# Polysketch attention into an ELU layer: the first keys in two loads of whole rows, the head in another order, sums read between the two ELU halves

## Chip, cores, metric

One core of one Trainium2 chip. The time is device microseconds for one execution of the whole program; the kernel before takes 302.09 us (median of 9 runs, 301.78 to 302.22).

## What is computed

```python
def phi(x):                                   # S1, S2: (8, 32)
    a = np.einsum('rd,bhsd->bhsr', S1, x)
    b = np.einsum('rd,bhsd->bhsr', S2, x)
    return np.einsum('bhsi,bhsj->bhsij', a, b).reshape(*x.shape[:-1], 64)
q_p, k_p = phi(q), phi(k)                     # q, k, v: (4, 4, 1088, 32)
kv  = np.einsum('bhsf,bhsd->bhfd', k_p, v)
z   = np.sum(k_p, axis=2)
x   = einsum('bhsf,bhfd->bhsd', q_p, kv) / (einsum('bhsf,bhf->bhs', q_p, z) + 1e-6)
x   = x.transpose(0, 2, 1, 3).reshape(4352, 128)
h   = x @ w_in                                # (128, 2048)
g   = where(h > 0, h, exp(min(h, 0)) - 1)
out = g @ w_out                               # (2048, 128)
```

Keys are summed over the whole sequence of a batch, so no query of a batch can be finished before all its keys are. S1, S2 and the two weight matrices arrive as 64-bit numbers and are turned into 32-bit ones on the chip.

## The kernel before

The 4352 tokens are 68 half tiles of 64. A *group* g holds eight of them (512 tokens; group 8 has half as many). The 2048 hidden columns are eight *pairs* cp of two 128-column blocks c. A *step* is one (group, pair).

**The loop.** In step n TensorE makes the hidden columns, `mm1(g, cp)` (L496, tile `h`, four buffers, two per step). ScalarE and VectorE make the ELU of each block: `elu_a` (two activations, L504 and L505, into `e`) and `elu_d` (L511, into `gg`). Two steps later `mm2` (L525) adds the pair's product into `o`, a tile with one buffer. After the last pair of a segment `fin1` reads `o` so that the next segment may write it: a ScalarE copy to `oT` (L538), a VectorE addition to `oT` (L534), or a VectorE transpose to `ob` (L545), followed by the stores. The groups 0 and 1 go in segments of pairs 0-1, 2-3 and 4-7, in turns, because their weights are still being prepared; each later group is one segment. The program is scheduled by hand: each engine executes its instructions in the order in which the code emits them. Attention work of the later batches and the preparation of later weights are put into given steps (`at` before the step's elu, `late` after it).

**Preparing weights.** A pair's 64-bit words are loaded to `raw` and turned into `W`, by `RA` (L101, VectorE), `RB` (L106, ScalarE) and `RC`, which is four VectorE passes: `round_c` (L114, L115), `round_d` (L119), `round_e` (L127; for later pairs two POOL passes, L124 and L125). Entry i of `order` says what is prepared: 0 is the w_in half of pair 0, 1 is all of pair 1, 2 is the w_out half of pair 0, 3 is pair 2, and so on.

**The head.** Before the loop, batch 0's keys are loaded (`hd_k`, L140-141), transposed in 32x32 blocks (`transp`, L247, to `kT`), and sent through: `KF` (feature matmuls L269, copy to `ab` L273), `KO` (outer product to `kp`, L253), `KA` (sums over the keys into `kv`, L296), `KC` (`kvz`, L307), `KZ1` (`zm`, L316) and `KZ2` (L323, L324: the sums of keys as query weights `SW`), `KS` (POOL copies to `kvS`, L331). `make_SX` (L242-243) makes a helper for `KZ2`. Each has three parts (key tiles 0-3, 4-7, 8) where a second index is given.

Group 0 of the queries has a path of its own, so as not to wait for `SW`: `q1_first` (L394), `q2_first`, `q4_first` (L411-412), `q5_first` (x0ps L427, then the division dn, xn L438-440, the transposes x0tp L445 and copies to `xg`, L447-448). Group 1 goes by the general path: `q1` (L363, copy to `abw` L368), `q2` (L375-384, ending with the outer product `qp`), `q4` (transposes L460, copies to `qpT` L461), `q5` (L475) and `q5_out` (copies to `xg`, L486 on ScalarE and L487 on VectorE). `keep_warm` (L216) is a matmul into a tile that nobody reads.

**Loads.** Nearly all are issued by SP in program order: the S matrices, k's first part, q's first half tiles, the w_in half of pair 0, v of batch 0 (two loads of 64 partitions), the rest of pairs 1 and 0, q's second part, then the further pairs and batches. ScalarE's queue takes S2 and k's second part.

The order of the head that the change rewrites is L566-611, and the loop's body L655-673.

Of the kernel before, what the change touches and what calls it, by code (L numbers as in the profile page):

```python
# [22 lines left out]
def _ap(ap: bass.AP, free):  # L23
    return dataclasses.replace(ap, ap=[list(ap.ap[0])] + [list(x) for x in free])
# [3 lines left out]
def kernel(  # L28
# [44 lines left out]
    def load_hd(eng, x, src, b, t0, t1):  # L73
        if (x, b) not in hd:
            hd[x, b] = work.tile([P, 2, NT, D], F32, name="hd_" + x, tag="hd_" + x)
        eng.dma_start(hd[x, b][:, :, t0:t1, :],
                      src[b].rearrange("h (a c t) d -> (h a) c t d", a=32, c=2)[:, :, t0:t1, :])

    def load_v(eng, b):
        for u in range(2):  # L80
            t0, t1 = u * KT, min(NT, u * KT + KT)
            r = slice(64 * u, 64 * u + 64)
            src = v[b].rearrange("h (y t) d -> y h t d", t=NT)[:, :, t0:t1, :]
            if b == 0:
                eng.dma_start(vt[b][r, :VN].rearrange("p (h t d) -> p h t d", h=H, t=KT)[:, :, :t1 - t0, :], src)
            else:
                for h in range(H):
                    eng.dma_start(vt[b][r, h * KT:h * KT + t1 - t0, :D], src[:, h])
# [45 lines left out]
    for x, (eng, src) in enumerate(((nc.sync, S1), (nc.scalar, S2))):  # L134
# [2 lines left out]
            eng.dma_start(raw_s[rs].rearrange("p c w -> p (c w)"), src.bitcast(U32))  # L137
        else:
            eng.dma_start(S16[rs, :], src)
    load_hd(nc.sync, "k", k, 0, 0, KT)  # L140
    load_hd(nc.scalar, "k", k, 0, KT, NT)
    warm = const.tile([R, 1], F32, name="warm")
    nc.vector.memset(warm[:], 0.0)
    nc.scalar.activation(warm[:], warm[:], EXP)
# [5 lines left out]
    def load_w(cp, i):  # L150

        f = slice(2 * cp * P, (2 * cp + 2) * P)
        src = moe_w_out[f, :].rearrange("(c p) d -> p c d", p=P) if i else moe_w_in[:, f]
        if wide:
            if cp not in raw_w:
                raw_w[cp] = work.tile([P, 4 * P, 2], U32, name="raw", tag="raw", bufs=6)
            src = src.bitcast(U32)
            to = raw_w[cp][:, 2 * P * i:2 * P * i + 2 * P, :].rearrange("p c w -> p (c w)")
        else:
            to = W[:, cp, 2 * P * i:2 * P * i + 2 * P]  # L160
        nc.sync.dma_start(to.rearrange("p (c f) -> p c f", f=src.shape[-1]) if i else to, src)
# [16 lines left out]
    def RC(i, pool=False):  # L178
        round_w(round_c, i)
        round_w(round_d, i)  # L180
        round_w(round_e, i, pool)

    load_w(0, 0)
    load_v(nc.sync, 0)
    load_w(1, 0)
    load_w(1, 1)
    load_w(0, 1)
    load_hd(nc.sync, "q", q, 0, 8, NT)
    for cp in range(2, NP):
        load_w(cp, 0)  # L190
        load_w(cp, 1)
# [34 lines left out]
    Sx = const.tile([2 * R, H, D], F32, name="Sx")  # L226
    nc.vector.tensor_copy(Sx[:], _ap(S16[:], [[0, H], [1, D]]))

    Sab = const.tile([FD, H, 2 * R], F32, name="Sab")
    SW = const.tile([FD, B, H, 3, R], F32, name="SW")  # L230
    keep_warm(3)
# [8 lines left out]
    def make_SX():  # L240
        xps = psum.tile([P, 512], F32, name="SXps", tag="aux")
        nc.tensor.matmul(xps[:, :FD], idr[:].rearrange("p x j -> p (x j)"), Sx[:R].rearrange("p h d -> p (h d)"))  # L242
        nc.scalar.copy(SX[:], xps[:, :FD])


    def transp(dst, x, b, t0, t1):
        nc.vector.transpose(dst[b][:, t0:t1, :].rearrange("p t (a c) -> p c t a", c=2), hd[x, b][:, :, t0:t1, :])  # L247


    def outer(dst, ab):  # L250
# [61 lines left out]
    def KZ1(b):  # L312

        zms[b] = work.tile([P, 2, 2, R], F32, name="zm", tag="zm")
        z_ = kvz[b][:, :, :, D] if b == 0 else kvz[b][:, :, 0, D:]
        (nc.vector if b == 0 else nc.gpsimd).tensor_mul(  # L316
            zms[b][:], _ap(z_, [z_.ap[1], z_.ap[2] if b == 0 else [0, 2], [0, R]]),
            _ap(zmask[:], [[0, 2], [R, 2], [1, R]]))

# [48 lines left out]
        nc.scalar.copy(abw[g][:, :H * n, :].rearrange("p (h t) y -> p h t y", h=H),  # L368
                       p[:, :n * 96].rearrange("p (t h y) -> p h t y", t=n, h=H))

    def q2(g):
        m = H * qn[g]
        x = abw[g][:, :m, :]
        pw = pws[g % 2]
        nc.vector.tensor_mul(pw[:, :m, :R], x[:, :, R:2 * R], x[:, :, 2 * R:])  # L375
        den = work.tile([P, 4 * H], F32, name="den", tag="den")
        nc.vector.tensor_reduce(den[:, :m], pw[:, :m], axis=AX, op=ADD)
        nc.vector.reciprocal(den[:, :m], den[:, :m])
        an = work.tile([P, 4 * H, R], F32, name="an", tag="an")
        nc.vector.tensor_mul(an[:, :m], x[:, :, R:2 * R], _ap(den[:, :m], [[1, m], [0, R]]))  # L380
        qp[g] = work.tile([P, 4 * H, R, R], F32, name="qp", tag="qp", bufs=2)
        a_ = an[:, :m]
        b_ = x[:, :, :R]
        nc.vector.tensor_mul(qp[g][:, :m], _ap(a_, list(a_.ap[1:]) + [[0, R]]),  # L384
                             _ap(b_, [b_.ap[1], [0, R], b_.ap[2]]))

# [25 lines left out]
    def q5_first():  # L414
        KC(0)
        KZ1(0)
        KS(0)
        round_w(round_c, 0)
        round_w(round_d, 0)
        keep_warm(2)  # L420
        xps = []
        for tt in range(2):
            p = psum.tile([P, 512], F32, name="x0ps", tag="h", bufs=4)
            xps.append(p[:, :8 * (D + 1)].rearrange("p (m d) -> p m d", d=D + 1))
            for m in range(4):
                t, g2 = 2 * tt + m // 2, m % 2
                nc.tensor.matmul(p[:, 2 * m * (D + 1):2 * (m + 1) * (D + 1)], qpT[0][:, t, g2, :],  # L427
                                 kvz[0][:, g2].rearrange("p w d -> p (w d)"), skip_group_check=True)
            if tt == 0:
                KZ2(0)  # L430
        round_w(round_e, 0)
        q1(1)
        keep_warm(1, P)
        dn = work.tile([P, 2, 8], F32, name="dn", tag="dn", bufs=1)
        xn = work.tile([P, 2, 8, D], F32, name="xn", tag="xn", bufs=1)
        xg[0] = work.tile([P, 512], F32, name="xg", tag="xg", bufs=2)
        for tt in range(2):
            nc.vector.tensor_scalar(dn[:, tt], xps[tt][:, :, D], 1e-6, None, op0=ADD)  # L438
            nc.vector.reciprocal(dn[:, tt], dn[:, tt])
            nc.vector.tensor_mul(xn[:, tt], xps[tt][:, :, :D], _ap(dn[:, tt], [[1, 8], [0, D]]))  # L440
        xt = []
        for tt in range(2):
            q = psum.tile([P, 512], F32, name="x0tp", tag="aux")
            for t in range(2):
                nc.tensor.transpose(q[:, t * P:t * P + P], xn[:, tt, 4 * t:4 * t + 4].rearrange("p m d -> p (m d)"), ident[:])  # L445
            xt.append(q)
        nc.scalar.copy(xg[0][:, :256], xt[0][:, :256])  # L447
        nc.vector.tensor_copy(xg[0][:, 256:], xt[1][:, :256])  # L448

    def q4(g):  # L450

# [37 lines left out]

    hs, es, gs, ops = {}, {}, {}, {}  # L490

    def mm1(g, cp):
        n = qn[g] * P
        hs[g, cp] = [psum.tile([P, 512], F32, name="h", tag="h", bufs=4) for c in range(2)]
        for c in range(2):
            nc.tensor.matmul(hs[g, cp][c][:, :n], W[:, cp, c * P:c * P + P], xg[g][:, :n])  # L496

    def elu_a(g, cp, c):

        n = qn[g] * P  # L500
        if c == 0:
            es[g, cp] = work.tile([P, 2, 512], F32, name="e", tag="e", bufs=2)
        e = es[g, cp][:, c, :n]
        nc.scalar.activation(e, hs[g, cp][c][:, :n], RELU, scale=-1.0)  # L504
        nc.scalar.activation(e, e, EXP, scale=-1.0)  # L505

    def elu_d(g, cp, c):
        n = qn[g] * P
# [2 lines left out]
        nc.vector.scalar_tensor_tensor(gs[g, cp][:, c, :n], es[g, cp][:, c, :n], -1.0, hs[g, cp][c][:, :n],  # L511
                                       op0=ADD, op1=MAX)

    def elu(g, cp):
        for c in range(2):
            elu_a(g, cp, c)
            elu_d(g, cp, c)

    def mm2(g, cp, first, last):
        n = qn[g] * P  # L520
# [43 lines left out]


    keep_warm(2)  # L566
    transp(kT, "k", 0, 0, KT)
    transp(kT, "k", 0, KT, NT)
    KF(0, 0)
    transp(qT, "q", 0, 0, 8)  # L570
    q1_first()
    KO(0, 0)
    KF(0, 1)
    KF(0, 2)
    q2_first()
    RA(0)
    RB(0)
    KO(0, 1)
    KO(0, 2)
    RA(1)  # L580
    RA(2)
    KA(0, 0)
    q4_first()
    make_SX()
    KA(0, 1)
    RB(1)
    RB(2)
    KA(0, 2)
    transp(qT, "q", 0, 8, NT)
    q5_first()  # L590
    mm1(0, 0)
    round_w(round_c, 1)
    round_w(round_d, 1)
    round_w(round_e, 1)
    for c in range(2):
        elu_a(0, 0, c)
    q2(1)
    mm1(0, 1)
    elu_a(0, 1, 0)
    for c in range(2):  # L600
        elu_d(0, 0, c)
    q4(1)
    round_w(round_c, 2)
    q5_out(1, q5(1, True))
    elu_a(0, 1, 1)
    round_w(round_d, 2)
    round_w(round_e, 2)
    for c in range(2):
        elu_d(0, 1, c)
    RA(3)  # L610
    RB(3)


# [41 lines left out]
    for n in range(N + 4):  # L655
        if 2 <= n < N:
            g, cp, first, last = steps[n]
            mm1(g, cp)
        for f, *a in extra.get(n, ()):
            f(*a)  # L660
        if 2 <= n < N:
            elu(g, cp)
        for f, *a in extra.get((n, 1), ()):
            f(*a)
        if 2 <= n < N + 2:
            g, cp, first, last = steps[n - 2]
            mm2(g, cp, first, last)
            if last:
                fin1(g, cp == NP - 1)
                if cp == NP - 1 and g == NQ - 1:  # L670
                    done[n + 2] = g
        if n in done:
            fin2(done[n])

# [28 lines left out]
```

## Time and profile before

| | us |
|---|---|
| median of 9 runs | 302.09 |
| the profiled execution | 301.81 |
| its span, first to last instruction | 299.5 |
| first key-feature matmul (L269) | 6.69 |
| last key-sum matmul, start of `kvz` (L307) | 14.29, 14.34 |
| first mm1 (group 0, pair 0) | 19.75 |
| first mm1 of the loop (group 1, pair 0) | 28.03 |
| last mm2 | 292.06 to 294.67 |

"Before" is one profiled execution; times are microseconds from the start of the span. A row of the chain of waits gives start, duration, engine, output tile, line and, behind an x, how many records were merged. A 32-bit matmul instruction leaves two records. `PEld` is TensorE's loading of weights, `SPq` the issuing of a DMA. In the slices of the page a digit is the busy share in tenths of 7.5 us. In a table by stretch the columns are busy time (and records) of PE, PEld, DVE, ACT and POOL, then the granted clock, the DMA share and GB/s. In the rows of one tile, three durations in ns are the least, the median and the greatest.

### The profile page before, as it was taken

Reading aid. Unit: us, or ns where it says so; the run is one execution under the profiler, and the core shown is the slowest. Engines: PE = TensorE matmul, PEld = TensorE weight load, DVE = VectorE, ACT = ScalarE, POOL = GpSimd, SP = SyncE. Lnnn points to the kernel's source line nnn. Section 1 sums busy time; section 2 is a strip of 40 time slices with the busy share of each in tenths; the row PEclk is TensorE's granted clock in tenths of the full one; section 3 lists DMA queues with packets and bytes.
Section 4 is the critical chain, followed back from the end, with each engine's and each line's share of the span. In section 5 each row is a group of like instructions: output and inputs, shape, how many; then the busy total and the mean of one; then the engine's idle time right before and its main releaser. Section 6 shows DMA issues by size and latency. Waiting matters only on the chain.

```text
span 299.5 us, 4046 instructions
## 1 busy us (share of the span) xinstructions
PE 287.8 (96%) x1454; PEld 147.5 (49%) x1454; DVE 168.7 (56%) x297; ACT 188.2 (63%) x354; POOL 18.5 (6%) x45
## 2 busy tenths in 40 slices
PE   8887999999998999999998999999999999999994
PEld 5763344544454653444544654445444544444682
DVE  5778899963765384436456175435433644354441
ACT  1536888566666268746657368656774687568581
POOL 2010034530000010000000010000000000000000
PEclk9999999999999999999999999999999999999999
DMA  6932999220010100001000200001001000110020
GB/s 191 335 120 77 205 215 215 30 74 0 9 29 0 28 10 0 2 10 26 2 1 6 31 0 0 0 14 23 0 0 24 14 0 1 15 23 0 4 32 18
DMA packets 38291, 13.37 MB, mean 45 GB/s; under 512 B 32768, under 2 KB 36480, under 8 KB 38272
## 3 DMA queue, kind: packets, MB, share of 16 engines
q1 hardware_dynamic: 37984, 12.86, 19.2%
q8 instruction: 11, 0.18, 0.3%
q10 hardware_dynamic: 288, 0.26, 0.3%
q14 instruction: 8, 0.07, 0.1%
HBM read 10.88 MB, written 2.23 MB: 44 GB/s over the span
## 4 chain that ended last, share of the span: by engine, by line
PE 92%; ACT 3%; DVE 3%; issue 1%; DVEq 0%
PE o L525 39%; PE h L496 37%; PE kv L296 3%; PE xps L475 2%; PE idle L216 2%; PE qtp L460 2%; PE abp L269 2%; PE abwp L363 2%; ACT e L505 1%; ACT e L504 1%; ACT ab L273 1%; PE x0ps L427 1%; DVE qp L384 0%; PE abqp L394 0%; DVE gg L511 0%
## 5 line engine op out<-in xcount | busy, mean ns | idle before, releaser
L511 DVE SCALAR_TENSOR_TENSOR gg<-e,h 128x512 f32<-128x512 f32 (+1 forms) x144 | 93.0, 655 | 105.8 <-ACT e L505 105.6
L525 PE MATMUL o<-gg,W 128*128 128x512 f32 (+1 forms) x288 | 130.7, 577 | 1.3 <-ACT oT L538 0.7
L496 PE MATMUL h<-xg,W 128*128 128x512 f32 (+1 forms) x288 | 128.8, 569 | 1.7 <-DVE xg L448 0.6
L504 ACT ACTIVATE e<-h 128x512 f32<-128x512 f32 (+1 forms) x144 | 81.5, 566 | 25.4 <-PE h L496 24.9
L505 ACT ACTIVATE e<-e 128x512 f32<-128x512 f32 (+1 forms) x144 | 87.3, 606 | 4.6
L496 PEld LDWEIGHTS h<-xg,W 128*128 128x128 f32 x288 | 54.5, 190 | 65.1 <-issue 55.9
L525 PEld LDWEIGHTS o<-gg,W 128*128 128x128 f32 x288 | 52.2, 190 | 54.8 <-issue 46.4
L368 ACT COPY abw<-abwp 128x384 f32<-128x384 f32 (+1 forms) x8 | 3.7, 459 | 28.4 <-PE abwp L363 28.4
L461 ACT COPY qpT<-qtp 128x512 f32<-128x512 f32 (+1 forms) x16 | 8.2, 562 | 17.1 <-PE qtp L460 17.1
L253 DVE TENSOR_TENSOR kp<-ab 128x1024 f32<-128x1024 f32 (+1 forms) x12 | 11.0, 943 | 5.8 <-ACT ab L273 5.8
L273 ACT COPY ab<-abp 128x256 f32<-128x256 f32 (+1 forms) x12 | 3.8, 317 | 12.9 <-PE abp L269 12.6
L296 PEld LDWEIGHTS kv<-v,kp 128*64 128x64 f32 (+1 forms) x288 | 9.1, 137 | 2.6 <-issue 1.5
L296 PE MATMUL kv<-v,kp 128*64 128x33 f32 (+3 forms) x288 | 9.9, 224 | 0.0
L486 ACT COPY xg<-xps 128x256 f32<-128x256 f32 (+1 forms) x8 | 2.9, 359 | 10.5 <-PE xps L475 10.5
L384 DVE TENSOR_TENSOR qp<-an,abw 128x1024 f32<-128x1024 f32 (+1 forms) x8 | 9.3, 1159 | 0.3
L460 PEld LDWEIGHTS qtp<-ident,qp 128*128 128x128 f32 x60 | 7.0, 143 | 4.0 <-issue 4.0
L460 PE MATMUL qtp<-ident,qp 128*128 128x128 f32 x60 | 8.0, 274 | 0.6 <-DVE qp L384 0.6
L269 PE MATMUL abp<-Sab,kT 128*64 128x64 f32 x136 | 6.7, 241 | 1.9 <-ACT ab L273 1.9
L269 PEld LDWEIGHTS abp<-Sab,kT 128*64 128x64 f32 x136 | 5.5, 153 | 5.4 <-ACT ab L273 2.4
L106 ACT ACTIVATE W<-W,ebias 128x512 uint32<-128x512 uint32 (+1 forms) x9 | 5.9, 669 | 3.4 <-DVE W L101 3.4
L475 PE MATMUL xps<-qpT,kvS 64*32 64x128 f32 (+2 forms) x200 | 7.7, 298 | 0.3 <-ACT qpT L461 0.3
L316 POOL TENSOR_TENSOR zm<-kvz,zmask 128x32 f32<-128x32 f32 x3 | 1.2, 392 | 108.3 <-issue 65.1
(84 smaller groups left out, 126.7 us busy)
## 6 DMA issues: line engine op xcount, KB each, us to landing
raw<-in_moe_w_in_dram SPq DMA_DIRECT2D x8, 256.0 KB, 5.5
raw<-in_moe_w_out_dram SPq DMA_DIRECT2D x8, 256.0 KB, 5.9
out_dram<-ob SPq DMA_DIRECT2D x104, 16.0 KB, 1.5
hd_k<-in_k_dram SPq DMA_DIRECT2D x3, 544.0 KB, 5.7
hd_q<-in_q_dram SPq DMA_DIRECT2D x3, 544.0 KB, 3.8
v<-in_v_dram SPq DMA_DIRECT2D x12, 72.0 KB, 5.4
v<-in_v_dram SPq DMA_DIRECT2D x12, 64.0 KB, 3.6
hd_k<-in_k_dram SPq DMA_DIRECT2D x1, 288.0 KB, 3.5
```

What stands on the lines that cost most here:

```text
L253: nc.vector.tensor_mul(dst, _ap(a_, list(a_.ap[1:]) + [[0, R]]), _ap(b_, [b_.ap[1], [0, R], b_.ap[2]]))
L269: nc.tensor.matmul(abp[64 * u:64 * u + 64, j * 64:j * 64 + 64], kT[b][:, u * KT + i, :], Sab[:].rearrange("p h y -> p (h y)"), skip_group_ ...
L296: nc.tensor.matmul(kv[64 * hp:64 * hp + 64, g2, :n], kp[:rows, j, h].rearrange("p i j -> p (i j)"), _ap(vt[b][:rows, off:off + D], [[VN - ...
L384: nc.vector.tensor_mul(qp[g][:, :m], _ap(a_, list(a_.ap[1:]) + [[0, R]]), _ap(b_, [b_.ap[1], [0, R], b_.ap[2]]))
L460: nc.tensor.transpose(p[:, o:o + P], qp[g][:, r:r + 2].rearrange("p t i j -> p (t i j)"), ident[:])
L461: nc.scalar.copy(qpT[g][:, 2 * hh:2 * hh + 2, :nh, :], p[:, :2 * nh * P].rearrange("p (h m s) -> p h m s", h=2, m=nh))
L475: nc.tensor.matmul(xp[w][D * h:D * h + D, :nh * P].rearrange("p (m s) -> p m s", s=P)[:, m0:m0 + m, s], kvS[64 * w:64 * w + 64, b, h, :], ...
L496: nc.tensor.matmul(hs[g, cp][c][:, :n], W[:, cp, c * P:c * P + P], xg[g][:, :n])
L504: nc.scalar.activation(e, hs[g, cp][c][:, :n], RELU, scale=-1.0)
L505: nc.scalar.activation(e, e, EXP, scale=-1.0)
L511: nc.vector.scalar_tensor_tensor(gs[g, cp][:, c, :n], es[g, cp][:, c, :n], -1.0, hs[g, cp][c][:, :n], op0=ADD, op1=MAX)
L525: nc.tensor.matmul(ops[g][:, :n], W[:, cp, (2 + c) * P:(3 + c) * P], gg[:, c, :n], start=(first and c == 0), stop=(last and c == 1))
```

## The change

Batch 0's keys come in two loads of 64 partitions (two heads each), one on SP and one on ScalarE's queue, with all of a partition's 34 key rows in one piece; before, each load took part of the key rows of all 128 partitions. On SP the order becomes v, the w_in half of pair 0, q's second part, then the weights of pairs 1 and 0. The first key transpose is emitted before `Sab`. `zm` of batch 0 goes to POOL. In the head the orders of the engines change as below; `q5_first` has no warming matmuls, its q transpose stands ahead of the division, and ScalarE makes both copies to `xg`. `q2(1)` makes its outer product in two parts; `mm1(0, 0)` and `elu_a` are emitted in parts; `mm1(0, 1)` comes after `q5(1)`. In the loop the last mm2 of a segment and its `fin1` are emitted between the ELU of block 0 and that of block 1; TensorE's order there stays the same.

```diff
-    load_hd(nc.sync, "k", k, 0, 0, KT)
-    load_hd(nc.scalar, "k", k, 0, KT, NT)
+    hd["k", 0] = work.tile([P, 2, NT, D], F32, name="hd_k", tag="hd_k")
+    for i, eng in enumerate((nc.sync, nc.scalar)):
+        eng.dma_start(hd["k", 0][64 * i:64 * i + 64].rearrange("p c t d -> p (c t d)"),
+                      k[0, 2 * i:2 * i + 2].rearrange("h (a x) d -> (h a) (x d)", a=32))
...
+    load_v(nc.sync, 0)
     load_w(0, 0)
-    load_v(nc.sync, 0)
+    load_hd(nc.sync, "q", q, 0, 8, NT)
     load_w(1, 0)
     load_w(1, 1)
     load_w(0, 1)
-    load_hd(nc.sync, "q", q, 0, 8, NT)
...
+    transp(kT, "k", 0, 0, KT)
...
-        (nc.vector if b == 0 else nc.gpsimd).tensor_mul(
+        nc.gpsimd.tensor_mul(
...
-    def q2(g):
+    def q2(g, parts=1):
...
+        for i in range(parts):
+            h = slice(i * m // parts, (i + 1) * m // parts)
...
         KC(0)
         KZ1(0)
         KS(0)
-        round_w(round_c, 0)
-        round_w(round_d, 0)
-        keep_warm(2)
+        RC(0)
+        KZ2(0)
...
-            if tt == 0:
-                KZ2(0)
-        round_w(round_e, 0)
-        q1(1)
-        keep_warm(1, P)
+        transp(qT, "q", 0, 8, NT)
...
-            xt.append(q)
-        nc.scalar.copy(xg[0][:, :256], xt[0][:, :256])
-        nc.vector.tensor_copy(xg[0][:, 256:], xt[1][:, :256])
+            nc.scalar.copy(xg[0][:, 256 * tt:256 * tt + 256], q[:, :256])
+            if tt == 0:
+                q1(1)
...
     keep_warm(2)
-    transp(kT, "k", 0, 0, KT)
     transp(kT, "k", 0, KT, NT)
     KF(0, 0)
     transp(qT, "q", 0, 0, 8)
-    q1_first()
     KO(0, 0)
     KF(0, 1)
+    q1_first()
     KF(0, 2)
-    q2_first()
+    make_SX()
+    KO(0, 1)
+    KO(0, 2)
     RA(0)
     RB(0)
-    KO(0, 1)
-    KO(0, 2)
+    q2_first()
+    for i in range(3):
+        KA(0, i)
+    q4_first()
+    q5_first()
+    mm1(0, 0, (0,))
     RA(1)
-    RA(2)
-    KA(0, 0)
-    q4_first()
-    make_SX()
-    KA(0, 1)
-    RB(1)
-    RB(2)
-    KA(0, 2)
-    transp(qT, "q", 0, 8, NT)
-    q5_first()
-    mm1(0, 0)
-    round_w(round_c, 1)
-    round_w(round_d, 1)
-    round_w(round_e, 1)
-    for c in range(2):
-        elu_a(0, 0, c)
-    q2(1)
-    mm1(0, 1)
-    elu_a(0, 1, 0)
+    RB(1)
+    elu_a(0, 0, 0, (0,))
+    q2(1, 2)
+    q4(1)
+    mm1(0, 0, (1,))
+    elu_a(0, 0, 0, (1,))
+    RC(1)
+    x1 = q5(1, True)
+    elu_a(0, 0, 1, (0,))
+    q5_out(1, x1)
+    elu_a(0, 0, 1, (1,))
+    mm1(0, 1)
+    RA(2)
+    RB(2)
     for c in range(2):
         elu_d(0, 0, c)
-    q4(1)
-    round_w(round_c, 2)
-    q5_out(1, q5(1, True))
-    elu_a(0, 1, 1)
-    round_w(round_d, 2)
-    round_w(round_e, 2)
+    for c in range(2):
+        elu_a(0, 1, c)
+    RC(2)
+    RA(3)
     for c in range(2):
         elu_d(0, 1, c)
-    RA(3)
     RB(3)
...
         if 2 <= n < N:
-            elu(g, cp)
+            elu(g, cp, 0)
+        if 2 <= n < N + 2:
+            g2, cp2, first, last = steps[n - 2]
+            if last:
+                mm2(g2, cp2, first, last)
+                fin1(g2, cp2 == NP - 1)
+                if cp2 == NP - 1 and g2 == NQ - 1:
+                    done[n + 2] = g2
+        if 2 <= n < N:
+            elu(g, cp, 1)
         for f, *a in extra.get((n, 1), ()):
             f(*a)
-        if 2 <= n < N + 2:
-            g, cp, first, last = steps[n - 2]
-            mm2(g, cp, first, last)
-            if last:
-                fin1(g, cp == NP - 1)
...
+        if 2 <= n < N + 2 and not last:
+            mm2(g2, cp2, first, last)
```

## The prediction

> **What bounds the kernel now.** I read the page's busy line and slices first, then the chain of work that ended last in order of time, then the DMA rates by stretch.
>
> ```profile
> PE 287.8 (96%) x1454; PEld 147.5 (49%) x1454; DVE 168.7 (56%) x297; ACT 188.2 (63%) x354; POOL 18.5 (6%) x45
> ...
> PE   8887999999998999999998999999999999999994
> ...
> DVE  5778899963765384436456175435433644354441
> ```
>
> TensorE is the bound from slice 5 on: steps of 1.72 us (mm1, L496) and 1.72 us (mm2, L525) follow each other. The change doesn't touch their number. So there are two places to win: the head, until the first loop step (mm1 of group 1, pair 0), and the few holes between loop steps. The chain shows the end of the head:
>
> ```profile
> 19.18 0.43 DVE xg L448
> 19.61 0.61 DVE W L114
> ...
> 23.37 1.23 DVE qp L384
> ...
> 24.74 0.64 PE qtp L460 x4
> ...
> 26.14 1.30 PE xps L475 x16
> ...
> 27.46 0.44 DVE xg L487
> ...
> 28.03 1.95 PE h L496 x4
> ```
>
> After the copy to xg of group 0, the chain runs through VectorE: four rounding passes of pair 1 (19.61 to 22.1), the q2 chain, then transposes, q5, a copy. TensorE waits for all this; the pair of matmuls mm1(0,1), which needs only pair 1's weights, sat early in the order and itself waited for the rounding. The first loop step starts at 28.03.
>
> The holes of the loop, from the same chain:
>
> ```profile
> 35.13 1.73 PE h L496 x4
> ...
> 36.91 0.58 ACT oT L538
> ...
> 37.53 1.99 PE o L525 x4
> ...
> 95.13 0.69 DVE gg L511
> 95.82 0.61 DVE oT L534
> ...
> 96.47 1.98 PE o L525 x4
> ...
> 162.12 0.72 DVE ob L545
> ...
> 162.88 1.98 PE o L525 x4
> ```
>
> The tile "o" has one buffer, so the next group's first mm2 waits until the sum was read. At 36.91 ScalarE reaches that copy only behind both elu halves; mm1 ended at 36.87 and mm2 starts at 37.53: 0.66 us. At 95.82 and 162.12 VectorE reaches it behind the second gg; mm2 would have been due at 96.20 and 162.58 (1.91 + 1.72 after 92.57 and 158.95): 0.27 and 0.30 us. Together 1.23 us. At the other seams nothing shows, because attention matmuls lie between.
>
> **The change part by part.** I count from K0, the first feature matmul of the keys (KF, L269): 6.69 us before.
>
> *Key loads.* Before, 288 KB on SP landed 3.5 us after 1.20 (4.70), 256 KB on ACT 4.1 us after 1.37 (5.47); the transposes ran 4.86 to 6.22. Each load now fills 64 partitions with rows of 4352 B, and the first transpose needs both. The rates by stretch (last columns: DMA share, GB/s):
>
> ```profile
> 4.00:4.50 0.50, 0.50 (x3) 0.42 (x2) 0.00 (x0) 0.00 (x0) 0.00 (x0) 1.00 1.08 385
> ...
> 7.00:7.50 0.50, 0.50 (x14) 0.50 (x14) 0.00 (x0) 0.00 (x0) 0.00 (x0) 1.00 1.04 236
> ...
> 8.50:9.00 0.50, 0.50 (x18) 0.50 (x16) 0.50 (x1) 0.36 (x1) 0.00 (x0) 1.00 1.05 225
> ...
> 10.00:10.50 0.50, 0.50 (x21) 0.50 (x22) 0.50 (x2) 0.21 (x1) 0.00 (x0) 1.00 1.10 350
> ```
>
> Around 7 to 9 us the queue serves batch 0's v, two loads of 64 partitions each, at 225 to 268 GB/s; weights over 128 partitions go at 350 to 385. The Trainium skill (SBUF — State Buffer, "Can I just issue two DMAs to hit both halves?") speaks against this edit: two concurrent loads, one to each half of the partitions, gain only 6% over a single one, since they share the same DMA engines. By the 128-partition row the 557 kB of k are there at about 4.8 (0.335 MB by 4.0, the rest at 370 GB/s, 0.2 to landing); by the rule, at the v rate of 245 GB/s, at about 5.35, and up to 5.9 if SP's q load mixes in. But here the halves come from two queues, and rows are four times longer. I take 5.3. Then transpose 0.77, Sab 0.22 behind it, transpose 0.67 and 0.1 of hand-over give K0 = 7.0 (+0.3; bounds 0, where the warming matmuls until 6.69 hold it, and +0.9).
>
> *Other loads.* On SP, v (544 KB) moves ahead of the first weights (256 KB), and the second q half ahead of pair 1's. v then lands some 0.7 us (256 KB at 350 to 385 GB/s) earlier than before (9.66: issued at 3.86, 5.8 to landing), and is wanted only at 10.2. First weights at about 9.7, wanted at 11.0; pair 1's some 0.8 us later than before, wanted at 17. The POOL memsets aren't passed. Nothing: the cover is over 0.5 us each.
>
> *Order until the first sum.* The row durations are 1.22 us for a kp or qp (starts 1.14 apart), 1.5 from K0 to the first kp. VectorE now does kp, kp, the small kp, RA(0) (0.29), qp: done at K0+5.4. TensorE: KF 1.05, then KF 0.7 and q1 0.6 (by the rows 0.62 to 0.85 each, and the clock rises there), KF and SX 0.7, all 72 KA together (2.4; batch 1's took 2.34) from 3.2 to 5.6. Before, kvz started at K0+7.65; now at 5.7. That is 1.95 won.
>
> *From kvz to the first mm1.* VectorE: kvz 0.29, all of RC(0) 1.7 (before, partly later), SW 0.19, then the q transpose 0.77 (before at 12.68, hidden), then the division chain 1.62: 10.1. zm moves to POOL: 0.29 to 0.69 us by its rows (0.19 on VectorE), but RC(0) covers it and kvS; uncovered it would cost at most 0.5. TensorE: x0tp of half 0 at 9.45, q1(1) 0.81, x0tp of half 1 at 10.6; ScalarE copies xg, abw (0.48), xg: 11.5. First half of mm1(0,0) at 11.6; before 13.06.
>
> *From there to the loop.* pw starts with abw, 11.2; 1.33 to the outer product, now two of 0.65: done 13.2 and 13.8. The split costs 0.06 and saves 0.6, since the first four transposes need the first half only. q4 13.35 to 14.55, second half of mm1(0,0) to 15.4, q5 to 16.3. RC(1) 2.53 us after 13.75: 16.3, then mm1(0,1) 16.4 to 18.15; xg of group 1 is ready at 16.9 and no longer on the path. First loop step at K0+18.15. Its mm2 needs RC(2): RA(2) 0.25, two gg 1.19 and RC(2) 1.7 after 16.85 end at 19.95: 0.2 late. So K0+18.35 against 28.03 − 6.69 = 21.34: 3.0 less the 0.3 of K0 is 2.7 us.
>
> VectorE is nearly gapless here, so I followed it on: RC(3), two gg, RC(4), gg(1,1) end at K0+28.7 and 29.25; mm1(0,3) needs the buffers at 28.9 and 29.7. Covered, by 0.2 to 0.4.
>
> *Seams in the loop.* No instruction is added; mm2, the copy or sum, and its DMAs move between the halves of elu. Behind the moved wait lies the second half (ScalarE's two activations, 1.2; VectorE's gg, 0.65), wanted two steps (6.9 us) later: nothing. At 36.91 the copy would start at about 35.8 and end at 36.4, before 36.85; at 95.82 the add would run 94.6 to 95.3, before 96.2. All 1.23 us go; what is late next is mm1, which doesn't wait. Bounds 0.6 (only the ScalarE seam) to 1.25.
>
> *Warming matmuls.* Five of 256 or 128 columns leave q5_first, three groups, where TensorE would wait anyhow: nothing, unless the clock falls (below).
>
> Sum: 2.7 + 1.2 = 3.9. The profiled execution took 301.81 (span 299.5 and 2.31 around it): 297.9. The runs' median is 302.09, 0.28 more: **298.2**.
>
> **Rivals.**
> 1. *VectorE becomes the bound, or k lands late.* Margins of 0.2 us in a gapless VectorE row are thin, and the skill's rule on halves may hold fully (k at 5.9). Each costs 0.6 to 1.2: 299.4. For it: VectorE's slices 5 to 8 at 8 to 9 tenths. Against: it is freed of an xg copy and its long waits (0.7, 0.8 and 1.0 us between 19 and 31).
> 2. *The seams don't close*: the holes shift, because the moved copy now waits for mm2 itself. Then only 2.7: 299.4. Against: mm2 ends 1.2 us or more before the copy or sum starts now (35.13 to 36.91, 160.86 to 162.12).
> 3. *Slower: the TensorE clock.* The slices' clock row shows full speed all along, but weight loads of one form don't:
>
> ```profile
> L269 PEld LDWEIGHTS abp<-Sab,kT x18: 182/227/231, 6.6 to 8.3; 128*64 128x64 f32 x18
> ...
> L269 PEld LDWEIGHTS abp<-Sab,kT x18: 133/160/227, 8.3 to 9.7; 128*64 128x64 f32 x18
> ```
>
> Until about 8.3 us TensorE ran at some 0.6 of its pace. The Trainium skill (TensorE: Matmul & The Clock Gate, "What's actually happening") says a window of about 3.4 us of idleness closes the clock to half. I count no hole above 1 us in the new head; before, holes of 0.6 us between matmuls (24.1 to 24.7, 27.4 to 28.0) didn't close it. By the rule nothing is lost; if the missing fillers or the later K0 do hold it at half through the head, KA costs 2 more, x0ps, q1 and mm1 of group 0 another 4, so 304. It turns to slower once over 3.9 us are lost on the path.
>
> **How the numbers follow.** My forecast (297.0 to 299.0): 0.58; rivals 1 and 2, alone or together (299.0 to 301.4): 0.29; better than 297: 0.04; within 0.2% (0.6 us, about what a measurement of this kernel can tell from no change): 0.03; rival 3: 0.06. The range 296.8 to 300.6 reaches from the forecast with all margins kept (1.0 better) over most of rivals 1 and 2. Faster 0.91.
>
> **What would show it.** k landing near 5.3 and KF at 7.0; kvz 5.7 us after KF; first mm1 11.6 after it, with two x0tp groups around q1(1); mm1(1,0) near 25.2; after it no idle VectorE until gg(1,1) and no TensorE wait for gg. In the loop: no wait of L525's successor for the oT or ob lines. Wrong would be: the weight loads of KA at 227 ns, KF after 7.9, or mm1(0,3) waiting for gg.

## The result and the profile after

| | before | after |
|---|---|---|
| median, us | 302.12 (30 runs) | 298.25 (10 runs, 297.53 to 300.37) |
| ratio | | 0.9883, interval 0.9861 to 0.9904 |
| profiled execution; its span | 301.81; 299.5 | 297.53; 295.7 |
| KF, start with all keys transposed | 6.69 | 7.62 |
| start of `kvz` | 14.34 | 13.39 |
| first mm1 | 19.75 | 19.03 |
| first mm1 of the loop | 28.03 | 25.69 |
| first key features of batch 1 (KF) | 44.67 | 41.71 |
| end of the last mm2 | 294.67 | 290.45 |

The change gives 3.87 us by the medians and 4.28 in the profiled executions. The last mm2 ends 4.22 earlier: 2.34 come from the head, 0.62 from the stretch between the first loop step and batch 1's KF (16.64 us before, 16.02 after), 1.26 from the rest. Of this rest the two later seams are 1.09 (below); the other 0.17 isn't traced. The profiled execution of after is the fastest of its ten; three of the ten took 300.08, 300.19 and 300.37. Experiments 5, 6 and 12 deal with these.

The page of after, first its busy line and slices, then the chain's shares by engine and the row of mm2:

```profile
PE 285.3 (97%) x1448; PEld 146.3 (49%) x1448; DVE 167.8 (57%) x296; ACT 188.1 (64%) x355; POOL 19.0 (6%) x46
...
PE   7979989999999999999999999999999999999993
...
DVE  5889999954558275436456274435442554355441
...
PE 86%; DVE 8%; DMA 2%; issue 1%; ACT 1%; ACTq 0%; DVEq 0%
...
L527 PE MATMUL o<-gg,W 128*128 128x512 f32 (+1 forms) x288 | 130.3, 576 | 0.0
```

mm2's last column, idle time before it, is 0.0: no seam waits. In the row of slices VectorE is at 8 to 9 tenths from slice 2 to slice 8. The head in the chain of waits of after:

```profile
1.35 4.69 DMA hd_k<-in_k_dram
...
6.07 0.78 DVE kT L233
...
7.62 1.80 PE abp L273 x29
...
10.95 2.42 PE kv L300 x72
13.39 0.30 DVE kvz L311
...
16.95 0.41 PE x0tp L445 x2
...
20.08 1.29 DVE qp L390 x2
...
23.23 0.69 DVE W L127
...
40.34 1.23 DVE kT L233
41.57 0.14 issue
41.71 1.17 PE abp L273 x32
```

The chain begins with ScalarE's half of the keys, which lands at 6.04. It then passes through VectorE in most of its steps until 41.57, where batch 1's key transpose releases batch 1's KF. TensorE's own row around the start of the loop (idle time and releaser in brackets):

```profile
23.97 3.70 PE L497 MATMUL h<-xg,W 128*128 128x512 f32 x8 [0.37 <-DVE W L127]
27.51 1.88 PE L527 MATMUL o<-gg,W 128*128 128x512 f32 x4
29.23 1.88 PE L497 MATMUL h<-xg,W 128*128 128x512 f32 x4
...
41.71 1.15 PE L273 MATMUL abp<-Sab,kT 128*64 128x64 f32 x32 [0.29 <-DVE kT L233]
```

The first row holds mm1(0,1) and mm1(1,0): the second starts 1.72 after 23.97. And the place of the seam that stood at 95.82 before, in the chain of after:

```profile
89.48 1.91 PE o L527 x4
91.39 1.72 PE h L497 x4
93.11 1.72 PE o L527 x4
```

Before, the third row came after a hole and took 1.98. So each hole had cost its own length and some 0.26 us in the matmuls behind it. The two views count this differently. In TensorE's row four records take 1.88 in a run and 1.98 behind a hole, but in a run the next four start 1.72 after these, so 0.16 overlaps; a hole takes the overlap away (0.16) and lengthens the row (0.10).

### The profile page after: what moved, and what is told of

It is laid out like the page before. It is cut to its first block, busy times and chain, and to the rows that moved or that the text cites. A ratio compares the mean times of both kernels' runs of the same rounds, so it can differ in the third digit from the quotient of the medians.

```text
span 295.7 us, 4034 instructions
## 1 busy us (share of the span) xinstructions
PE 285.3 (97%) x1448; PEld 146.3 (49%) x1448; DVE 167.8 (57%) x296; ACT 188.1 (64%) x355; POOL 19.0 (6%) x46
## 4 chain that ended last, share of the span: by engine, by line
PE 86%; DVE 8%; DMA 2%; issue 1%; ACT 1%; ACTq 0%; DVEq 0%
PE o L527 38%; PE h L497 35%; PE kv L300 3%; PE abwp L367 2%; PE abp L273 2%; PE xps L475 2%; PE qtp L460 2%; DVE gg L514 2%; DMA hd_k<-in_k_dram 2%; DVE W L114 1%; DVE raw L119 1%; DVE kT L233 1%; DVE raw L115 1%; DVE W L101 1%; DVE qp L390 0%
## 5 line engine op out<-in xcount | busy, mean ns | idle before, releaser
L124 POOL TENSOR_TENSOR raw<-raw,tiny 128x512 f32<-128x512 f32 x4 | 5.3, 1316 | 32.0 <-DMA hd_q<-in_q_dram 24.5
```

## The experiments

Each is compared with a before of 302.04 to 302.08. The intervals of the ratios are 0.4 to 1.1 us to each side, so a difference of some 0.5 us between two experiments rests on what the traces show. The edits are made on after or, where said, on experiment 4's kernel, which turned out the fastest. Every stretch of the computation is present in all of them; experiment 8 adds a pass that nobody reads.

**1. The loop's part alone**, on the kernel before: only the last mm2 and `fin1` between the two elu halves.

```diff
-            elu(g, cp)
+            elu(g, cp, 0)
+            if last:
+                mm2(g2, cp2, first, last)
+                fin1(g2, cp2 == NP - 1)
+            elu(g, cp, 1)
```

> The kernel before with only the loop's reordering (last mm2 of a segment and its fin1 between the two elu halves). The prediction's sum: the three holes of 0.66, 0.27 and 0.30 us close, so 1.2 us less than before. A second reading, from the two traces: behind each hole the first mm2 also took 0.26 us longer (1.98 instead of 1.72), so that closing them is worth 2.0 us. Rival (the holes only shift): no change. In the trace, mm2 of the next group should follow mm1 without a wait at all three places.

Measured: 300.09 (22 runs), ratio 0.9932 (0.9912 to 0.9952): 2.0 us faster. The first seam in TensorE's row:

```profile
35.79 1.88 PE L524 MATMUL o<-gg,W 128*128 128x512 f32 x4
37.51 1.88 PE L496 MATMUL h<-xg,W 128*128 128x512 f32 x4
39.22 1.88 PE L524 MATMUL o<-gg,W 128*128 128x512 f32 x4
```

Three rows 1.72 apart, no bracket: the hole is gone and comes back nowhere, so "the seams don't close" falls. (The profiled execution is one of two long ones, 302.46 and 302.97; its head was slow, the rows here are not.) The 2.0 fits the second reading, holes plus refill: 1.23 + 3 x 0.26 = 2.0.

**2. The head's part alone**: after, with the loop body of before.

> The changed kernel with the old loop: head and loads of the change alone. The changed kernel's trace starts the loop at 25.69 instead of 28.03; if head and loop add up, this is 1.2 to 2.0 us above the changed kernel, some 1.9 to 2.6 us below the one before. If the head's gain only counts because the loop keeps up, more is lost than that. The three holes should be back, 2.3 us earlier.

Measured: 302.04 (13 runs), ratio 0.9979 (0.9959 to 1.0). The runs fall into two sets: three of 299.13 to 300.24, as expected, and ten of 301.59 to 302.48. The profiled one is of the second set. A row of its TensorE:

```profile
38.08 1.98 PE L528 MATMUL o<-gg,W 128*128 128x512 f32 x4 [0.66 <-ACT oT L541]
```

The hole is back with its full 0.66 and its refill of 1.98. KA's weight loads, in the groups of the first 17 us (busy us, mean ns, idle):

```profile
L300 PEld LDWEIGHTS kv<-v,kp 128*64 128x64 f32 (+1 forms) x72 | 4.0, 224 | 0.3 <-DVE kp L257 0.2
```

They took 224 ns each. In after's profile the same row is:

```profile
L300 PEld LDWEIGHTS kv<-v,kp 128*64 128x64 f32 (+1 forms) x72 | 2.3, 137 | 0.2
```

So in this execution TensorE kept its slow pace until about 16 us. KA started 0.99 later than in after and took 4.31 instead of 2.46, so it ended 2.8 later. As a measure of the head's worth the run is inconclusive, but it shows that rival 3's event happens, at a price of 2 to 3 us and not of 6. A better measure of the head is after against experiment 1, which differ only in the head and its loads: 298.25 against 300.09, 1.84 us, where 2.7 was predicted.

**3. Keys loaded as before**, all else as after.

```diff
-    for i, eng in enumerate((nc.sync, nc.scalar)):
-        eng.dma_start(hd["k", 0][64 * i:64 * i + 64].rearrange("p c t d -> p (c t d)"),
-                      k[0, 2 * i:2 * i + 2].rearrange("h (a x) d -> (h a) (x d)", a=32))
+    load_hd(nc.sync, "k", k, 0, 0, KT)
+    load_hd(nc.scalar, "k", k, 0, KT, NT)
```

> The changed kernel with the loads of k as before (each load over all 128 partitions, pieces of 1.1 kB). Theory (the two halves cost time, as the measured landing at 6.04 says): k is there by 5.5, KF starts at 6.7 to 6.9 instead of 7.6, and since the chain runs on from there without slack the time falls by 0.7 to 0.9 us. Rival (another wait hides it, or the q and v loads become late instead): no change within 0.2 us.

Measured: 297.16 (4 runs, 297.12 to 297.21), ratio 0.9838 (0.9825 to 0.9851): 1.1 us faster than after. The first part lands at 4.7, the second at 5.4, KF starts at 6.78. The key edit costs time.

**4. All keys in one load of 128 partitions, whole rows**, on SP.

```diff
-    for i, eng in enumerate((nc.sync, nc.scalar)):
...
+    load_hd(nc.sync, "k", k, 0, 0, NT)
```

> The changed kernel with k in one load of whole rows over 128 partitions on SP. If it is the halves of the partitions that make k late, this lands at about 4.9 and is as fast as the old loads or 0.1 to 0.3 us better: 0.7 to 1.1 us below the changed kernel. If it is the long rows of 4.35 kB, it lands at about 6 like the changed kernel, with no gain. If the ScalarE queue alone was late, it lands near 4.9 as well, and a run with both halves on SP must tell.

Measured: 296.84 (5 runs, 296.60 to 296.97), ratio 0.9824 (0.9812 to 0.9837). It is 1.4 us faster than after and beats both kernels. The key tile over the first 10 us, with its time to landing, in after:

```profile
L143 SPq DMA_DIRECT2D hd_k<-in_k_dram x1: 564/564/564, 1.2 to 1.2; - x1
L143 ACTq DMA_DIRECT2D hd_k<-in_k_dram x1: 542/542/542, 1.3 to 1.3; - x1
...
DMA to landing us min/median/max: 3.6/4.2/4.7
```

And the same in this kernel:

```profile
L76 SPq DMA_DIRECT2D hd_k<-in_k_dram x1: 380/380/380, 1.2 to 1.2; - x1
...
DMA to landing us min/median/max: 3.6/3.6/3.6
```

One load of 557 kB lands in 3.6 us, at 4.8. Of the halves only one does; the other needs 4.7. TensorE of this kernel:

```profile
6.80 1.98 PE L270 MATMUL abp<-Sab,kT 128*64 128x64 f32 x32
...
23.33 1.98 PE L494 MATMUL h<-xg,W 128*128 128x512 f32 x4 [0.37 <-DVE W L127]
...
41.05 1.15 PE L270 MATMUL abp<-Sab,kT 128*64 128x64 f32 x32 [0.28 <-DVE kT L230]
```

KF starts some 0.8 earlier than in after, now held by the warming matmuls and not by the keys; mm1(0,1), at 23.33 against 23.97, gains 0.64, and batch 1's KF 0.66.

**5. A third warming group ahead of KF**, on after: `keep_warm(2)` becomes `keep_warm(3)`, to fill the hole that the late keys leave.

> The changed kernel with one more warming matmul ahead of KF, so that TensorE has no hole between 6.8 and 7.6 us. Theory (hole): some executions of the changed kernel take 2.2 us more, and 10 of 13 with the old loop, because the hole makes TensorE's pace rise one window later, as the profile of e2 shows (weight loads of KA at 227 instead of 138 ns). Then this one has no such executions: all near 298.1 to 298.3. Rival (chance, or the late keys themselves): the share of slower executions stays at a quarter or more, 300.2 or above.

Measured: 297.43 (4 runs, 297.16 to 297.93), ratio 0.9849 (0.9829 to 0.9869): 0.8 faster than after, no long execution. In its profile the weight loads of KF take 137 ns on average instead of 215: the pace had risen before KF. But the hole was not filled:

```profile
4.52 1.56 PE L219 MATMUL idle<-some 128*128 128x256 f32 x6
7.36 0.33 PE L273 MATMUL abp<-Sab,kT 128*64 128x64 f32 x2 [1.27 <-DVE Sab L242]
```

At the full pace the six filler records were done at 6.08, and TensorE then stood idle for 1.27, longer than in after (0.23). The keys landed at 6.39. So in this execution the pace had risen before there was a hole, and the hole didn't lower it; mm1(0,1) came at 23.82, 0.15 earlier than in after.

**6. One warming group fewer ahead of KF**, on experiment 4: `keep_warm(2)` becomes `keep_warm(1)`, meant to make a hole like after's while the keys land early.

> The version with k in one load (e4, 296.84, no slower execution in 5) with one warming matmul less ahead of KF: TensorE idle from about 5.75 to 6.85, KF as early as before. Hole theory: a large share of executions at 2.2 to 2.7 us more (299 to 299.5), the weight loads of KA at 227 ns in such a trace. Rival (late keys): all at 296.8.

Measured: 296.91 (6 runs), ratio 0.9849 (0.9816 to 0.9883). Four runs of 296.01 to 296.99, two of 298.89 and 298.92. In the profiled execution (296.99) the first pair of KF's records follows the fillers at once and the rest starts at 6.49, so the hole is under 0.2 us and not the 1.1 expected. The share of long executions goes from none of five to two of six, which so few runs can't establish.

**7. Both halves of the keys on SP**, on after: `(nc.sync, nc.scalar)` becomes `(nc.sync, nc.sync)`.

> The changed kernel with both halves of k on SP's queue. If two halves of the partitions cost bandwidth by themselves (245 GB/s as for v), k lands at 5.2 to 5.4, KF starts at 7.0 to 7.1, and the time is 0.5 us below the changed kernel: 297.7. If only ScalarE's queue got too small a share, k lands at 4.8 to 4.9 as in e4: 296.9.

Measured: 298.29 (6 runs), ratio 0.9887 (0.9855 to 0.9918): the same as after. The tile's row:

```profile
L143 SPq DMA_DIRECT2D hd_k<-in_k_dram x2: 564/576/587, 1.2 to 1.8; - x2
...
DMA to landing us min/median/max: 3.8/4.1/4.3
```

The halves land at 5.0 and 6.1, the second as late as ScalarE's did. So it isn't ScalarE's queue that makes the keys late, and they came later than the expectation had them. The profiled execution, 300.03, is a long one.

**8. One more VectorE pass ahead of RC(1)**, on experiment 4: a 128x512 product into a tile that nobody reads.

```diff
+    dummy = const.tile([P, 512], F32, name="dummy")
+    nc.vector.tensor_mul(dummy[:], _ap(some[:], [[0, 2], [1, 256]]), _ap(some[:], [[0, 2], [1, 256]]))
     q4(1)
```

> The version of e4 with a VectorE pass of 128x512 added ahead of RC(1), whose result nobody reads. Theory (VectorE is the bound from kvz to the first batch-1 key transpose, as the chain of the changed kernel says): its 0.67 us appear nearly in full, 0.6 to 0.7 more: 297.5. Rival (TensorE's order sets the head and VectorE has slack): less than 0.2 more.

Measured: 298.71 (6 runs), ratio 0.9885 (0.9858 to 0.9912), in two sets: 297.34, 297.65, 297.97, and 299.45 to 299.50. The middle of the first set is 0.8 above experiment 4. TensorE:

```profile
23.74 3.70 PE L494 MATMUL h<-xg,W 128*128 128x512 f32 x8 [0.95 <-DVE W L127]
```

The wait for W grows from 0.37 to 0.95, by 0.58: about a pass. VectorE is the bound there. That half of the runs were long, without a hole ahead of KF, speaks against the hole as the only cause (the profiled execution, 297.34, is of the short half).

**9. The division ahead of the rounding**, on experiment 4: q transpose and SW first, the rounding passes in the gaps of the division chain.

> The version of e4 with VectorE's order behind kvz changed: q transpose first, then SW, then the division, with the passes of RC(0) in the gaps in which the division waits for x0ps. By e4's trace VectorE waits 0.82 us for abw at 17.3 to 18.1; now q1(1) comes some 0.45 us earlier and that wait shrinks to nothing. Theory (VectorE's chain from kvz on is the bound): 0.4 to 0.5 us less than e4, 296.4. Rival (x0ps on TensorE sets the place of the division): within 0.15 of e4.

Measured: 297.04 (5 runs), ratio 0.9832 (0.9796 to 0.9867): no gain; one of the five is long, 298.86. VectorE of this kernel:

```profile
15.26 0.17 DVE L436 TENSOR_SCALAR dn<-x0ps 128x8 f32<-128x8 f32 x1 [0.35 <-PE x0ps L430]
```

The division now waits for x0ps. Here TensorE, not VectorE's order, sets its place: x0tp starts at 16.27 against 16.32.

**10. The outer product of q2(1) in one piece**, on experiment 4: `q2(1, 2)` becomes `q2(1)`.

> The version of e4 with the outer product of q2(1) in one piece. The prediction: the split saves 0.6 us on the way to q4. The other reading, from the changed kernel's trace: the way to the loop leads through RC(1), which starts 0.06 us earlier without the split, while q5 ends 0.6 later, 0.2 to 0.3 behind the end of RC(1): 0.2 to 0.3 more than e4.

Measured: 297.36 (6 runs, 297.00 to 297.51), ratio 0.9834 (0.9804 to 0.9864): 0.5 slower than experiment 4. TensorE of this kernel:

```profile
20.55 1.06 PE L457 MATMUL qtp<-ident,qp 128*128 128x128 f32 x8 [1.30 <-DVE qp L387]
...
23.02 3.27 PE L494 MATMUL h<-xg,W 128*128 128x512 f32 x7
```

The transposes wait 1.30 instead of 0.76. But mm1(0,1) follows the first x0tp (16.05) by 6.97 us, against 7.01 in experiment 4: up to there the later q4 was absorbed. The cost stands on VectorE, in the row that copies q5's result behind RC(1), here and in experiment 4:

```profile
23.20 0.42 DVE L484 COPY xg<-xps 128x256 f32<-128x256 f32 x1 [0.28 <-PE xps L472]
```

```profile
23.19 0.42 DVE L484 COPY xg<-xps 128x256 f32<-128x256 f32 x1
```

Without the split VectorE waits 0.28 for q5. It leads on to batch 1's KF, which follows the first x0tp by 25.05 (41.10) instead of 24.73 (41.05). That is 0.32, as the second reading of the expectation had it; the rest of the 0.5 isn't in the profiles.

**11. The warming matmuls back in `q5_first`**, on experiment 4.

```diff
         KZ2(0)
+        keep_warm(2)
...
                 q1(1)
+                keep_warm(1, P)
```

> The version of e4 with the warming matmuls back in the first path (two ahead of x0ps, one behind q1). The prediction holds that leaving them out is worth nothing and costs nothing: two records of 256 columns each are 0.5 us ahead of x0ps, beside qpT's copy and the VectorE chain, so within 0.3 us of e4. Rival 3 (they keep the clock up): less time than e4, or fewer long executions.

Measured: 297.78 (5 runs, 297.67 to 297.87), ratio 0.9846 (0.9816 to 0.9876): 0.94 slower than experiment 4. TensorE:

```profile
10.62 2.46 PE L297 MATMUL kv<-v,kp 128*64 128x64 f32 x72
...
14.16 1.11 PE L216 MATMUL idle<-some 128*128 128x256 f32 x4
15.11 1.90 PE L430 MATMUL x0ps<-kvz,qpT 128*128 128x66 f32 x16
```

x0ps starts 4.49 after KA's start, against 3.73 (10.26 to 13.99) in experiment 4: the filler stands 0.76 us in its way. Of this 0.49 is left at mm1(0,1) (24.18, 13.56 after KA's start, against 13.07). KA itself started 0.36 later than in experiment 4, before any of these fillers, so that not all of the 0.94 can be put down to them.

**12. No warming matmuls ahead of KF**, on experiment 4: `keep_warm(3)` and `keep_warm(2)` become `keep_warm(0)`.

> The version of e4 without any warming matmuls ahead of KF. Rival 3's mechanism by itself: TensorE begins its work at half pace at KF and stays there for a window[...]; KF and q1 take 0.5 us more and KA 2.0 us more where it lasts that long. Expected 1.5 to 2.6 us above e4 in most executions (298.4 to 299.4), KA's weight loads at 227 ns. If the pace doesn't depend on earlier work, 296.8.

Measured: 297.87 (6 runs), ratio 0.9858 (0.982 to 0.9896), in two sets: 297.00, 297.12, 297.17, and 298.58, 299.18, 299.73. The profiled execution is of the second. KA in its TensorE row:

```profile
10.63 4.30 PE L297 MATMUL kv<-v,kp 128*64 128x64 f32 x72
```

KA's weight loads in its first 17 us:

```profile
L297 PEld LDWEIGHTS kv<-v,kp 128*64 128x64 f32 (+1 forms) x72 | 4.0, 224 | 0.3 <-DVE kp L254 0.2
```

KA takes 4.30 instead of 2.46. Yet in half the executions the time is that of experiment 4 plus 0.2 to 0.3, so even here the pace is no certain loss.

## Why the prediction was right, and where it wasn't

The total was right, 298.25 against 298.2, and so was the mechanism: a shorter head and closed seams. That it came so close is luck. Several terms were mis-sized, and their errors cancel: the head gave less than predicted, the seams more.

**K0, the key loads: too small.** Predicted: keys at 5.3, K0 +0.3, bounds 0 to +0.9. Measured: 6.04, and KF from 7.62, +0.93. I had weighed the Trainium skill's rule (SBUF — State Buffer, "Can I just issue two DMAs to hit both halves?") and taken less than the v rate that stood for it, on the ground of two queues and longer rows. Experiment 7 shows that two queues are no gain (6.1 from one queue). Experiment 4 shows the reverse of the edit at work: one load over all partitions lands at 4.8. The rates of after, by stretch:

```profile
4.00:4.50 0.50, 0.40 (x3) 0.33 (x2) 0.06 (x1) 0.00 (x0) 0.00 (x0) 1.00 1.01 244
4.50:5.00 0.50, 0.50 (x3) 0.46 (x3) 0.00 (x0) 0.00 (x0) 0.00 (x0) 1.00 0.90 174
```

These are 244 and 174 GB/s where before had 385 and 365, with the DMA share about 1: the engines were busy and moved less. A stretch counts all loads in flight, though, and experiment 4 too has 225 and 224 there, when its keys are nearly in. The trace's packets are clearer. In experiment 4 a packet of 4352 B takes 168 ns (median). In after SP's half, which came first, has 172, and ScalarE's, which came second, 297; in experiment 7 it is 168 and 301. And ScalarE's last packet was done at 5.27 but landed at 6.04, 0.77 later, against 0.36 in experiment 4 (4.39, 4.75). So the second half and the landing are late, and not both halves equally; why is not shown.

Beside experiment 4 this term costs after 1.4 us by the medians and 0.64 at mm1(0,1) in the two profiles. The profiled execution of after is its fastest, and without its three long ones the middle of the other seven is still 298.12, 1.28 above experiment 4. That further half microsecond is in no profile here, but it goes with the granted clock: of the five executions of 298.08 to 298.53 four have a mean of 0.991, the two below 298 have 0.999 and 1.0, and in experiment 7 the two at 298.26 and 298.33 have 0.991 again. So it can't all be put down to the keys. The three long ones have 0.995 and 0.996, so the clock's mean is not what makes them long.

**Other loads, "nothing": nearly.** Each was given a cover of over 0.5 us, and in after none is waited for. v came near it: in experiment 10, where TensorE's pace rose early, KA waited 0.17 for v and started at 9.97.

**The order of the head: right.** From KF on, kvz was predicted 5.7 later and came 5.77 later, the first mm1 11.6 and 11.41, the first loop step 18.15 and 18.07 (25.69 − 7.62), its mm2 0.2 late and 0.10 late.

**The seams: too small.** Predicted 1.23, measured 2.0 in experiment 1. That they close was right, and no instruction behind them became late. What failed is the count of a hole by its wait alone. Each of the three left another 0.26 in the four records behind it (1.98 or 1.99 instead of 1.72); so did the hole ahead of the first loop step of before (1.95, now gone: 0.23).

**VectorE "covered, by 0.2 to 0.4": partly wrong.** mm1(0,3) doesn't wait, but batch 1's KF, a step that I hadn't followed VectorE to, does. It was due at 41.27 (27.51 and eight steps of 1.72) and came at 41.71. With this the stretch adds up: 0.66 + 0.27 for the first seam, 0.23 for the first step, less 0.10 and 0.44, are the 0.62 measured. Experiment 8 shows the bound itself: a pass added to VectorE comes out as 0.58 of wait for TensorE and 0.8 in the time. So both mechanisms of rival 1 came true, VectorE's in part, and the seams paid for them.

**Warming matmuls, "nothing": wrong.** In the new order TensorE doesn't wait where they stood, and they would stand ahead of x0ps on the path. Put back they cost up to 0.94, of which the trace shows 0.76 at x0ps and 0.49 at mm1(0,1). This belongs to the gain of the head, in which I counted x0ps without them. The count was off too: three matmuls leave `q5_first`, in two groups (TensorE's records go from 1454 to 1448), not five in three.

**The split, "saves 0.6": half of it shown.** q4 comes 0.54 earlier (1.30 less 0.76), but RC(1) hides a part; experiment 10 has 0.5 by the medians and 0.32 in its profile, by way of VectorE's copy and not of q4.

**Rival 3, the pace of TensorE: partly true.** A part of the executions keeps the slow pace until 14 to 16 us instead of 8 to 10 and is some 2 to 2.7 us longer. Its price was put at 6 and is less, since what follows KA was not slow for so long; it can't make the change slower than before. After's median lies 0.72 above its profiled execution, where I had taken before's 0.28. So my sum of 3.9 fell 0.38 short of the 4.28 in the profiled executions, and the medians gave it back; that is part of the luck. The pace explains little of the 0.72: without the three long executions the median is only 0.13 lower. The rest goes with the granted clock above, and its cause is not shown.

What decides the pace stays open. The pace is seen only in profiled executions (of the long ones those of 1, 2, 7 and 12); the others are counted as long by their times. Kernels with a hole ahead of KF (after, 2, 6, 7) had 17 long executions of 35; those meant to have warming matmuls up to KF had few (1: 2 of 22; 3, 4, 5, 10, 11: none of 24; 9: 1 of 5), except experiment 8 with 3 of 6; no warming at all (12) gave 3 of 6. Before itself has 10 of 87 above 303. The hole goes with a larger share and isn't the whole cause. In the profiles of 5 and 10 there was a hole as well, of 1.27 and 0.59 us, once the pace had risen, and the pace stayed.

## What to carry to other kernels

Price a hole on the bounding engine with what comes behind it, not only by its wait: here 0.26 us on top of 0.27 to 0.66. Split a load by rows over all partitions, not by partitions (here the keys were in at 4.8 or 5.4, not at 6.04). When an order is rewritten, look for the fillers that now stand on the path. After each local gain, follow the engine that the gain leaned on to its next deadline: VectorE's came some 16 us after the first loop step.

## What the runs showed of the hardware

- Of two loads of 64 partitions the second to run was slow, in two queues (after) as in one (experiment 7): 297 and 301 ns for a packet of 4352 B, against 168 in one load of 128 partitions (experiment 4). The 544 KB landed 4.8 and 4.9 us after the first issue, against 3.6.
- A 128x64 32-bit weight load takes 224 to 227 ns until TensorE's pace rises and 137 ns after it, while the profile's clock row shows full speed in both. In the profiles of these kernels the rise came between 4.2 us (experiment 5) and about 16 us (experiment 2); after, with the same head as experiment 2, had it at about 9. The Trainium skill (TensorE: Matmul & The Clock Gate, "What's actually happening") tells of a free-running window of about 3.4 us and calls the number of slow matmuls variable from run to run. That it varies, these runs agree with; the spread of some 12 us is wider than one window.
- A hole on TensorE of 0.27 to 0.66 us cost 0.26 us beyond its wait: the next four 512-column records took 1.98 us, where in a run four start every 1.72.
